# Attention pairs laid out anew: score units, row maxima, additions and softmax pieces of a mixture kernel

## Chip, cores and metric

The kernel runs on one core of a Trainium2 chip. The metric is device time in microseconds (us), the median of 3 runs. TensorE (PE) multiplies matrices, VectorE (DVE) reduces and does elementwise work, ScalarE (ACT) does exponentials and copies, GpSimd (POOL) does elementwise work between SBUF tiles, SyncE (SP) issues the DMAs in order. All engines run their own instruction queue in program order and wait for each other by semaphores.

## The reference, cut to what matters

```python
q_pool = q.reshape(B, H, S // 2, 2, D).mean(axis=3)      # B, H, S, D = 4, 8, 1152, 64
scores = (1 / np.sqrt(D)) * np.matmul(q_pool, k.transpose(0, 1, 3, 2))
scores = scores - np.max(scores, axis=-1, keepdims=True)
attn = np.exp(scores)
attn = attn / (np.sum(attn, axis=-1, keepdims=True) + 1e-09)
x = np.matmul(attn, v)            # then heads side by side: x is [2304, 512]
...
logits = x @ phi                  # 8 experts of 4 slots: softmax over tokens (d), over slots (c)
slot_input = d.T @ x
slot_out[e] = np.maximum(slot_input[e] @ w1[e], 0.0) @ w2[e]
y = c @ slot_out
...
xn = y / np.sqrt(np.mean(y * y, axis=-1, keepdims=True) + 1e-06) * rms_g
out = (silu(xn @ w_gate) * (xn @ w_val)) @ w_out
```

The gated layer's weights come as 64-bit numbers. Inputs q, k and phi are drawn eight times larger than the rest.

## The kernel before, in words

The 32 heads are handled in 16 pairs, p = 0 to 15. For a pair, the keys come in 9 tiles of 128 (kt) and the 576 pooled queries in two halves h of 288. One **score unit** (`qk`) multiplies a key tile with a half of the queries, for both heads at once: the high and low parts of k and q in three products, and a fourth (`pick` by `mr`) that adds minus the row maximum. ACT takes the exponential (`e`), `add_e` adds the tiles up for the softmax denominator (`acc`), and `av` multiplies them with the values. Row maxima of the next pair are found beforehand: a **maximum item** (`max_item`, 11 or 14 in a pair) multiplies q and k into two PSUM banks (`mxp`) and DVE reduces them (`mx`). `max_red` joins the pieces, `max_row` turns the column of maxima into a row on PE (`mxt`) and copies it on ACT (`mrow`), and `send_row` sends it by four small DMAs into `mr`, where the next pair's first score unit reads it.

Score units, maximum items and nearly all other products of this stage share three PSUM buffers of two banks each (`two_banks`), used in turn; a product waits until the reader of the buffer's last tenant is done. Two further banks hold the value products.

The order on every engine is written out by hand. For each pair the loop goes through its steps u: 9 steps of both halves, or, for pair 0 (`HALVED`), 18 steps, the first half's nine and then the second's. Within a step a short list such as `STEP` gives the order of score units (q), maximum items (m), additions (e) and, in every third step, a **visit**, the value products of the last three key tiles (a, b, c). `MAX`, `MAX_1` and `MAX_0` say how many maximum items each step may take. All other work is hung in by time: the tables `AT`, `AT_0` (pair 0), `AT_01` and `AT_15` give each piece a place such as 5.8 (within step 5, at eight tenths of its list), and `side` sorts them.

```python
while todo and todo[0][0] <= now + i / len(order) / len(steps) * 9:
    todo.pop(0)[2]()
```

Pieces that matter here: `round_k` and `high_q` (ACT) round k and q to their high parts, `low_k` and `low_q` (DVE) take the rest; `block_q` (ACT) fills the small stack `tb` for the last 64 rows of queries; `sum_q` (POOL) pools the queries. `load_64`, `abs_64` (ACT) and `turn_64` (DVE, called a **turn** below) fetch a block of 64-bit weights and make it 32-bit; `spill` sends it back to memory. `c_turn`, `c_exp`, `c_sum`, `c_out` make the softmax over slots, in pairs 6 and 7, 10 and 11, 14 and 15, and once after the pairs. `sums`, `recips` and `inverse` make the denominators of the pair before, `x_turn`, `x_divide`, `x_logits`, `logit_add` and `d_turn` its output and logits. `kraw`, `qraw`, `vt`, `kh`, `kl` and the raw 64-bit blocks share a pool of 11 buffers (A). After the pairs come the experts and the gated layer, which the change does not touch.

Of the kernel before, what the change touches and what calls it, by code (L numbers as in the profile page):

```python
# [13 lines left out]
AF = mybir.ActivationFunctionType  # L14
ALU = mybir.AluOpType
AX = mybir.AxisListType
PSUM = bass.MemoryType.PSUM

NP = 16
# [4 lines left out]
NBK = 6  # L24
TB = 96
# [4 lines left out]

STEP = "q0 m q1 m e0 e1".split()
STEP_V = "q0 q1 m e0 e1 a m m b c".split()
STEP_0 = "q m m e a b c".split()
VISIT = 3
PART = 6
MAX = [0, 0, 3, 0, 0, 3, 0, 0, 3]
MAX_1 = [1, 1, 3, 1, 0, 3, 0, 0, 3]
NMAX = 9
AHEAD = 3
AT = dict(  # L40
# [13 lines left out]
    recips=2.87,  # L54
    c_turn=8.74,
    c_exp=0.9,
    c_soft=[6.5, 8.9],
    pair_up=6.6,
    inverse=[3.4, 4.0],
    turn_64=[0.9, 5.8, 5.81],  # L60
    low_q=3.2,
    high_q=5.51,
    block_q=5.52,
# [17 lines left out]
    load_15=[0.5, 1, 1.5, 2, 2.5, 3, 3.5, 4, 4.5, 5.5, 5.84, 6, 6.5, 7, 7.5, 8, 8.5],  # L81
)
AT_0 = dict(
    max_tail=[2.85, 2.86],
    load_v=7.3,
    round_k1=[1.06, 1.56],
    block_q1=2.6,
    low_k=[1.3, 1.8],
    low_q=2.3,
    high_q=6.19,  # L90
    block_q=8.95,
    round_k=[7.91, 8.72],
    max_red=8.6,
    max_row=8.78,
    send_row=8.79,
    load_q=4.3,
    load_k=5.73,
    sum_q=5.91,
)
AT_01 = dict(  # L100
    x_turn=8.85,
# [1 line left out]
    drop_x=8.88,  # L103
    d_exp=8.84,
)
AT_15 = dict(
    x_turn=5.8,
    x_divide=[5.81, 5.82],
# [1 line left out]
    sums_a=8.55,  # L110
    inverse_a=[8.56, 8.57],
)
MAX_0 = [2, 1, 1, 1, 1, 0, 1, 1, 1, 1, 1, 1, 1, 1, 1, 1, 0, 0]
HALVED = (0,)
SQ_DVE = (0, 2)
SP_ACT = (1, 5, 4, 3, 2)
# [28 lines left out]
def attention_softmoe_gated_kernel(ctx: ExitStack, tc: tile.TileContext, kT, qT, vv, ip, cst, w1, w2, wg, wv, wo, rg, out):  # L145
# [263 lines left out]

    def add_e(p, kt, h):  # L410

        j = int(kt >= PART)
        n, e = kt - PART * j, ets[p, kt, h]
        if n == 0:
            first[p, h, j] = e
            return
        if n == 1:
            acc[p, h, j] = B([128, 2, HQ], F32, "acc")
        eng = dv if p in (0, NP - 1) and kt % 2 == 0 else gp
        eng.tensor_tensor(out=acc[p, h, j], in0=first[p, h, j] if n == 1 else acc[p, h, j], in1=e, op=ALU.add)  # L420

    def av(p, kt, h):
# [185 lines left out]
        ac.activation(ct[b], ct[b], AF.Exp)  # L608

    def c_sum(b):  # L610
        sm = csum[b] = S([TB, NBK], "csm")
        dv.reduce_sum(out=sm, in_=ct[b], axis=AX.X)
        ac.activation(sm, sm, AF.Copy, bias=1e-9)
        dv.reciprocal(sm, sm)

    csum = {}

# [101 lines left out]
    def side(p):  # L719
        n, m, l = p + 1, p + 2, p - 1  # L720
        todo = []

        def at(name, g):
            ts = (AT_0 if p == 0 else AT_15 if p == NP - 1 else AT_01 if p > 1 and p % 4 < 3 else AT).get(name, AT.get(name))
            for i, t in enumerate(ts if isinstance(ts, list) else [ts]):
                todo.append((t, len(todo), (lambda i=i: g(i))))

        if p == 0:
            at("round_k1", lambda i: round_k(1, i))
            at("block_q1", lambda i: block_q(1))  # L730
        if n < NP:
            at("low_k", lambda i: low_k(n, slice(576 * i, 576 * i + 576)))
            at("low_q", lambda i: low_q(n))
            at("load_v", lambda i: load_v(n))
            if p:
                at("max_tail", lambda i: max_item(n, NMAX + i))
            at("max_red", lambda i: max_red(n))
            at("max_row", lambda i: max_row(n))
            at("send_row", lambda i: send_row(n))
        if m < NP:  # L740
            at("load_q", lambda i: load_q(m))
            at("load_k", lambda i: load_k(m))
            at("sum_q", lambda i: sum_q(m))
            at("high_q", lambda i: high_q(m))
            at("block_q", lambda i: block_q(m))
            at("round_k", lambda i: round_k(m, i))
        if l >= 0:
            at("take_x", lambda i: take_x(l))
            at("sum_up", lambda i: sum_up(l, 1 - i))
            at("sums", lambda i: sums(l))  # L750
            at("recips", lambda i: recips(l))
            at("x_turn", lambda i: x_turn_all(l))
            at("x_divide", lambda i: x_divide(l, range(3 * i, 3 * i + 3)))
            at("drop_x", lambda i: rel("B"))
            at("inverse", lambda i: inverse(l, i))
            at("x_logits", lambda i: x_logits(l))
            at("logit_add", lambda i: logit_add(l))
            if p % 4 == 0 and p < NP - 1:
                at("d_turn", lambda i: dpart.__setitem__(("d", l // 4), (d_turn(l // 4), d_neg(l // 4))))
                at("d_exp", lambda i: d_exp(l // 4, *dpart.pop(("d", l // 4))))  # L760
            if p % 4 == 1 and p > 1:
                b = p // 4 - 1
                at("d_back", lambda i: d_back(b))
                at("d_copy", lambda i: d_copy(b))
                at("slot_part", lambda i: slot_part(b))
                at("slot_copy", lambda i: slot_copy(b))
                at("slot_turn", lambda i: slot_turn(b, pt[:, b]))
            if p % 4 == 2 and p > 2:
                b = p // 4 - 1
                at("c_turn", lambda i: c_turn(b))  # L770
            if p % 4 == 3 and p > 3:
                b = p // 4 - 1
                at("c_exp", lambda i: c_exp(b))
                at("c_soft", lambda i: (c_sum, c_out)[i](b))
        if p == 2:
            at("pair_up", lambda i: pair_up())
        if 0 < p < NP - 2:
            at("load_64", lambda i: load_64() if i < 2 or p % 2 or p < 8 else None)
            at("load_ew", lambda i: load(1, 99, KEEP_C + min(len(doubles), 4 * HELD + HELD_O)) if p >= FIRST_EW else None)
        if p < NP - 1:  # L780
            at("spill", lambda i: spill())
            at("abs_64", lambda i: abs_64(1))
            at("turn_64", lambda i: turn_64(1))
        if p == NP - 2:
            spill()
            assert not doubles
            at("load_14", lambda i: (keep_b.__setitem__(0, KEEP[3]), load(1, KEEP_A[0])))
        if p == NP - 1:
            at("sums_a", lambda i: sums(p))
            at("inverse_a", lambda i: inverse(p, i))  # L790
            at("load_15", lambda i: (keep_b.__setitem__(0, KEEP[0]), load(1, KEEP_A[1])))
        return sorted(todo, key=lambda x: x[:2])

    with tc.manual_schedule():
# [47 lines left out]
        def next_max(p, mx):  # L842
            if p == 0:
                mx += 9
                if mx < 14:
                    max_item(0, mx)
                    if mx == 13:
                        max_red(0)
                        max_row(0)
                        send_row(0, 3)  # L850
                else:
                    max_item(1, mx - 14)
            elif p == 1:
# [5 lines left out]
        for p in range(NP):  # L859
# [2 lines left out]
            steps = [(kt, h) for h in range(2) for kt in range(NKT)] if p in HALVED else [(kt, None) for kt in range(NKT)]  # L862
            for u, (kt, h) in enumerate(steps):
                now = u / 2 if p in HALVED else u
                order = STEP_0 if h is not None else STEP_V if kt % VISIT == VISIT - 1 else STEP
                quota = min(sum((MAX_0 if p == 0 else MAX_1 if p == 1 else MAX)[:u + 1]),
                            0 if p == NP - 1 else NMAX - AHEAD if p == NP - 2 else 99)
                for i, step in enumerate(order):
# [206 lines left out]
        c_turn(3)  # L1075
        c_exp(3)
        c_sum(3)
        c_out(3)
        for e in range(NE):
            pull()  # L1080
# [214 lines left out]
```

## Time and profile before

| | |
|---|---|
| median of 3 runs | 730.64 us (730.15 to 731.27) |
| profiled execution | 732.41 us, its span 730.3 us |
| busy: PE, DVE, POOL, ACT | 693.3, 478.9, 430.7, 393.6 us |
| pairs 0 to 15 | from 16.31 us to about 473 us of the span |
| a pair from 2 to 14 | 26 to 30 us |

Times in the profile are counted from the start of the span. A matmul's busy time includes its pipeline, so starts tell more than durations: in the timeline a row merges instructions of one kind that follow each other, gives the start, the length and how often, and in brackets the idle time of its engine just before and what ended it. PE is busy for 95% of the span, so most of what there is to see lies in short stops of PE and in stretches at the lower clock.

### The profile page before, as it was taken

The numbers are of one execution on the slowest core, as the hardware profiler recorded it, in microseconds if no ns is written. First come the engines' busy times: TensorE is split into PE (matmuls) and PEld (weight loads), VectorE is DVE, ScalarE is ACT, GpSimd is POOL, SyncE is SP. The second block draws the span as 40 slices with busy tenths as digits, with TensorE's granted clock in tenths as the row PEclk, the third lists the DMA queues.
The fourth block names the chain that finished last, engine by engine and source line by source line (L and its number), as shares of the span: only waits on it lengthen the run. The fifth ranks groups of instructions, "written<-read, shape, count | busy, mean of one in ns | idle before, by whom it ended". The sixth has DMA issues, their size and how long they took to land.

```text
span 730.3 us, 15136 instructions
## 1 busy us (share of the span) xinstructions
PE 693.3 (95%) x5924; PEld 484.6 (66%) x5924; DVE 478.9 (66%) x668; ACT 393.6 (54%) x828; POOL 430.7 (59%) x347
## 2 busy tenths in 40 slices
PE   4989999999999899999999999879999999999998
PEld 2666676666666566666666667434367888888887
DVE  5868898897797797788888775531064755534420
ACT  2455666656656666565665545342166865454320
POOL 5338788778687587686787775321026855535320
PEclk9999999999999999999999999979999999999999
DMA  5212633844835716527416317379990100000010
GB/s 176 98 57 98 213 115 115 285 140 147 282 112 178 247 54 243 190 68 272 145 41 243 104 47 263 114 245 373 388 353 1 44 15 29 30 30 29 15 37 35
DMA packets 52853, 103.53 MB, mean 142 GB/s; under 512 B 5816, under 2 KB 19632, under 8 KB 52784
## 3 DMA queue, kind: packets, MB, share of 16 engines
q1 hardware_dynamic: 52784, 102.59, 40.5%
q8 instruction: 46, 0.75, 0.4%
q14 instruction: 23, 0.19, 0.1%
HBM read 89.39 MB, written 13.11 MB: 140 GB/s over the span
## 4 chain that ended last, share of the span: by engine, by line
PE 78%; DVE 12%; DMA 4%; ACT 3%; issue 2%; POOL 1%; SPq 0%; DVEq 0%; ACTq 0%
PE yo L1198 21%; PE sc L403 18%; PE av L426 17%; PE mxp L346 4%; PE gv L1150 3%; DVE mx L347 3%; DVE kl L310 3%; DVE w L710 2%; PE hin L966 2%; DMA kraw<-in_kT_dram 2%; PE xo L488 2%; PE so L989 2%; PE sums L451 1%; PE mxp L356 1%; DVE mx L353 1%
## 5 line engine op out<-in xcount | busy, mean ns | idle before, releaser
L420 POOL TENSOR_TENSOR acc<-acc,e 128x576 f32<-128x576 f32 x148 | 207.9, 1433 | 37.2 <-ACT e L405 32.6
L405 ACT ACTIVATE e<-sc 128x576 f32<-128x576 f32 x288 | 165.0, 656 | 77.3 <-PE sc L403 76.7
L347 DVE TENSOR_REDUCE mx<-mxp 128x2 f32<-128x1024 f32 x120 | 143.5, 1221 | 62.7 <-PE mxp L346 62.7
L426 PE MATMUL av<-e,vt 128*64 128x288 f32 x1152 | 166.7, 417 | 0.0
L420 POOL TENSOR_TENSOR acc<-e 128x576 f32<-128x576 f32 x64 | 97.3, 1539 | 92.0 <-ACT e L405 91.8
L426 PEld LDWEIGHTS av<-e,vt 128*64 128x64 f32 x1152 | 73.4, 137 | 63.6 <-issue 27.6
L403 PE MATMUL sc<-qh,kh 64*128 64x288 f32 x576 | 95.4, 326 | 4.7 <-ACT e L405 3.9
L1198 PE MATMUL yo<-woh,hA 128*128 128x512 f32 (+1 forms) x312 | 98.9, 384 | 0.0
L403 PE MATMUL sc<-mr,pick 64*128 64x288 f32 x576 | 87.1, 295 | 1.9 <-DMA mr<-mrow 1.9
L403 PE MATMUL sc<-qh,kl 64*128 64x288 f32 x576 | 86.5, 295 | 0.0
L403 PE MATMUL sc<-ql,kh 64*128 64x288 f32 x576 | 86.5, 294 | 0.0
L1155 DVE SCALAR_TENSOR_TENSOR th<-th,gv 128x384 f32<-128x384 f32 x72 | 39.9, 554 | 62.5 <-ACT th L1152 61.8
L1181 POOL TENSOR_TENSOR hA<-hu,hA 128x384 fp32r<-128x384 f32 x48 | 48.7, 1016 | 42.7 <-ACT hA L1180 39.0
L403 PEld LDWEIGHTS sc<-qh,kh 64*128 64x128 f32 x576 | 55.0, 186 | 26.5 <-issue 7.4
L1198 PEld LDWEIGHTS yo<-woh,hA 128*128 128x128 f32 x312 | 57.6, 188 | 10.2 <-issue 0.7
L1152 ACT ACTIVATE th<-gv 128x384 f32<-128x384 f32 x72 | 35.2, 489 | 42.6 <-PE gv L1150 38.6
L1198 PE MATMUL yo<-wol,hA 128*128 128x512 f32 (+1 forms) x151 | 57.9, 383 | 0.0
L403 PEld LDWEIGHTS sc<-mr,pick 64*128 64x128 f32 x576 | 55.8, 187 | 2.4 <-DMA mr<-mrow 2.4
L403 PEld LDWEIGHTS sc<-qh,kl 64*128 64x128 f32 x576 | 55.7, 189 | 0.3
L403 PEld LDWEIGHTS sc<-ql,kh 64*128 64x128 f32 x576 | 55.6, 187 | 0.0
L346 PE MATMUL mxp<-kh,qh 64*128 64x512 f32 x240 | 48.8, 438 | 0.0
L1157 DVE SCALAR_TENSOR_TENSOR hu<-th,gv 128x384 f32<-128x384 f32 x72 | 39.9, 554 | 8.4 <-DVE th L1155 0.5
(190 smaller groups left out, 1065.4 us busy)
## 6 DMA issues: line engine op xcount, KB each, us to landing
w<-in_w_dram SPq DMA_DIRECT2D x86, 256.0 KB
w<-in_w_dram SPq DMA_DIRECT2D x21, 512.0 KB
vt<-in_vv_dram SPq DMA_DIRECT2D x16, 576.0 KB
qraw<-in_qT_dram SPq DMA_DIRECT2D x15, 576.0 KB
kraw<-in_kT_dram SPq DMA_DIRECT2D x15, 576.0 KB
away<-w SPq DMA_DIRECT2D x32, 256.0 KB
w<-away SPq DMA_DIRECT2D x32, 256.0 KB
raw<-in_wg_dram SPq DMA_DIRECT2D x12, 512.0 KB
```

What stands on the lines that cost most here:

```text
L310: eng.tensor_tensor(out=kl[p][:, c], in0=kraw[p][:, c], in1=f(kh[p][:, c]), op=ALU.subtract)
L346: pe.matmul(o[:, s, :], lhsT=q[r, 128 * t:128 * t + 128], rhs=k[r, 512 * c:512 * c + 512], start=True, stop=True)
L347: dv.reduce_max(out=heads[:, :, t, c], in_=o, axis=AX.X)
L403: pe.matmul(o[:, s, 0:HQ], lhsT=w[r, wk], rhs=q[r, c], start=(i == 0), stop=(i == 3))
L405: ac.activation(ets[p, kt, h], o[:, :, 0:HQ], AF.Exp, scale=0.0625)
L420: eng.tensor_tensor(out=acc[p, h, j], in0=first[p, h, j] if n == 1 else acc[p, h, j], in1=e, op=ALU.add)
L426: pe.matmul(avt[p, h][64 * s:64 * s + 64, 0:HQ], lhsT=vt[p][:, kt, 64 * s:64 * s + 64], rhs=ets[p, kt, h][:, s], start=(kt == 0), stop=(kt ...
L1152: ac.activation(t, o[0], AF.Tanh, scale=0.5)
L1155: dv.scalar_tensor_tensor(out=t, in0=t, scalar=1.0, in1=o[0], op0=ALU.add, op1=ALU.mult)
L1157: dv.scalar_tensor_tensor(out=u, in0=t, scalar=0.5, in1=o[1], op0=ALU.mult, op1=ALU.mult)
L1181: gp.tensor_tensor(out=b, in0=u, in1=f(a), op=ALU.subtract)
L1198: pe.matmul(o, lhsT=x, rhs=w[:, c], start=(ft == 0 and i == 0), stop=(ft == NF - 1 and i == 2))
```

## The change

Pair 0: the lists become "q e" for two steps and "q e m a m m b m c" for the third, so that three score units follow each other and all maximum items lie in the visits (`MAX_0`). All additions of pair 0 go to GpSimd (before, every second key tile's went to VectorE). The row of pair 0 itself is turned at the step after its second visit (`row_0`), not in the step of its last item; `round_k1`, `block_q1`, `low_k`, `low_q`, and the maxima of pair 1 (`max_red`, `max_row`, `send_row`) get other places. Pair 1: the twelve items lie in the visits but for one (`MAX_1`, `STEP_1`), and `max_red` comes at 5.83. All pairs: the accumulator of the first half is split after key tile 5 instead of 6 (`PART`); `c_sum` becomes three pieces at their own places (sum on DVE, guard on ACT, inverse on DVE); of the turns that stood at 5.8 and 5.81 one goes to 0.91 of the next pair, except in pairs 5, 9 and 13; pairs 8 and 10 may fetch a third 64-bit block.

```diff
 STEP = "q0 m q1 m e0 e1".split()
 STEP_V = "q0 q1 m e0 e1 a m m b c".split()
-STEP_0 = "q m m e a b c".split()
+STEP_1 = "q0 q1 m e0 e1 a m m b m c".split()
+STEP_0 = "q e".split()
+STEP_0V = "q e m a m m b m c".split()
-PART = 6
+PART = 5, 6
-MAX_1 = [1, 1, 3, 1, 0, 3, 0, 0, 3]
+MAX_1 = [0, 1, 4, 0, 0, 4, 0, 0, 3]
...
 AT = dict(
...
-    c_soft=[6.5, 8.9],
+    c_soft=[3.45, 5.505, 6.5, 8.52],
...
-    turn_64=[0.9, 5.8, 5.81],
+    turn_64=[0.9, 0.91, 5.8],
...
 AT_0 = dict(
-    max_tail=[2.85, 2.86],
     load_v=7.3,
-    round_k1=[1.06, 1.56],
-    block_q1=2.6,
-    low_k=[1.3, 1.8],
-    low_q=2.3,
-    high_q=6.19,
-    block_q=8.95,
-    round_k=[7.91, 8.72],
-    max_red=8.6,
-    max_row=8.78,
-    send_row=8.79,
+    round_k1=[0.6, 1.6],
+    block_q1=1.62,
+    low_q=2.1,
+    row_0=2.97,
+    low_k=[3.6, 5.1],
     load_q=4.3,
     load_k=5.73,
     sum_q=5.91,
+    high_q=6.19,
+    max_red=7.3,
+    max_row=7.48,
+    send_row=7.49,
+    round_k=[7.6, 8.6],
+    block_q=8.95,
 )
...
+AT_1 = dict(AT_01, turn_64=[0.9, 5.8, 5.81])
+AT_P1 = dict(max_red=5.83)
...
-MAX_0 = [2, 1, 1, 1, 1, 0, 1, 1, 1, 1, 1, 1, 1, 1, 1, 1, 0, 0]
+MAX_0 = [0, 0, 4, 0, 0, 4, 0, 0, 3, 0, 0, 3, 0, 0, 2, 0, 0, 0]
...
-        j = int(kt >= PART)
-        n, e = kt - PART * j, ets[p, kt, h]
+        j = int(kt >= PART[h])
+        n, e = kt - PART[h] * j, ets[p, kt, h]
...
-        eng = dv if p in (0, NP - 1) and kt % 2 == 0 else gp
+        eng = dv if p == NP - 1 and kt % 2 == 0 else gp
...
     def c_sum(b):
-        sm = csum[b] = S([TB, NBK], "csm")
-        dv.reduce_sum(out=sm, in_=ct[b], axis=AX.X)
-        ac.activation(sm, sm, AF.Copy, bias=1e-9)
-        dv.reciprocal(sm, sm)
+        csum[b] = S([TB, NBK], "csm")
+        dv.reduce_sum(out=csum[b], in_=ct[b], axis=AX.X)
+
+    def c_guard(b):
+        ac.activation(csum[b], csum[b], AF.Copy, bias=1e-9)
+
+    def c_inverse(b):
+        dv.reciprocal(csum[b], csum[b])
...
-            ts = (AT_0 if p == 0 else AT_15 if p == NP - 1 else AT_01 if p > 1 and p % 4 < 3 else AT).get(name, AT.get(name))
+            ts = (AT_0 if p == 0 else AT_15 if p == NP - 1 else AT_P1 if p == 1 else AT if p % 4 == 3 else AT_1 if p % 4 == 1 else AT_01).get(name, AT.get(name))
...
+            at("row_0", lambda i: (max_row(0), send_row(0, 3)))
...
-                at("c_soft", lambda i: (c_sum, c_out)[i](b))
+                at("c_soft", lambda i: (c_sum, c_guard, c_inverse, c_out)[i](b))
...
-            at("load_64", lambda i: load_64() if i < 2 or p % 2 or p < 8 else None)
+            at("load_64", lambda i: load_64() if i < 2 or p % 2 or p < 11 else None)
...
                     if mx == 13:
                         max_red(0)
-                        max_row(0)
-                        send_row(0, 3)
...
-                order = STEP_0 if h is not None else STEP_V if kt % VISIT == VISIT - 1 else STEP
+                if kt % VISIT < VISIT - 1:
+                    order = STEP if h is None else STEP_0
+                else:
+                    order = STEP_0V if p == 0 else STEP_1 if p == 1 else STEP_V
```

## Rows read from the trace of the kernel before

**Rows 1.** Waits of PE, whole span: us in total, times, longest us

```profile
PE sc L403 <- ACT e L405: 3.9, 2, 2.2
PE lgt L531 <- DVE mx L347: 2.8, 3, 0.9
...
PE sc L403 <- DMA mr<-mrow: 1.9, 2, 1.4
...
PE lgt L599 <- POOL acc L420: 1.0, 1, 1.0
...
PE xo L488 <- DVE mx L347: 0.9, 1, 0.9
PE lgt L599 <- DVE mx L347: 0.9, 1, 0.9
```

**Rows 2.** Windows of pairs 0, 1, 2, and two short ones: busy by engine, PEclk, DMA

```profile
16.31:48.00 31.69, 29.86 (x256) 19.77 (x256) 24.40 (x30) 15.36 (x29) 13.02 (x9) 1.00 0.16 57
48.00:79.79 31.79, 29.59 (x273) 20.23 (x271) 25.21 (x28) 17.29 (x33) 21.29 (x16) 0.95 0.39 131
79.79:106.08 26.29, 26.29 (x268) 18.00 (x267) 22.70 (x26) 17.32 (x34) 21.93 (x18) 1.00 0.42 133
...
51.66:55.06 3.40, 3.40 (x29) 3.26 (x27) 2.36 (x2) 1.83 (x4) 0.85 (x1) 0.50 0.96 330
242.85:246.25 3.40, 3.40 (x15) 1.40 (x14) 1.67 (x2) 2.98 (x10) 3.40 (x4) 0.51 0.93 297
```

**Rows 3.** Timeline of pair 7: start, length, engine, line, tiles, count, idle before

```profile
241.09 0.21 ACT L613 ACTIVATE csm<-csm 96x6 f32<-96x6 f32 x1 [2.24 <-DVE csm L612]
...
241.88 0.40 PE L403 MATMUL sc<-qh,kh 64*128 64x288 f32 x2 [2.19 <-ACT e L405]
```

**Rows 4.** Timeline of pair 3 at its last visit, and of pair 9 there

```profile
129.95 3.47 DVE L347 TENSOR_REDUCE mx<-mxp 128x2 f32<-128x1024 f32 x3
...
131.22 0.86 PE L488 MATMUL xo<-cs,xu 128*96 128x128 f32 x6 [0.94 <-DVE mx L347]
...
300.32 1.23 DVE L347 TENSOR_REDUCE mx<-mxp 128x2 f32<-128x1024 f32 x1 [1.98 <-PE mxp L346]
```

**Rows 5.** Durations by line: count, then ns minimum/median/maximum

```profile
L310 DVE TENSOR_TENSOR kl<-kraw,kh x30: 744/748/1989, 23.3 to 439.3; 128x576 fp32r<-128x576 f32 x30
...
L710 DVE SCALAR_TENSOR_TENSOR w<-w,raw x36: 672/683/1898, 71.3 to 436.8; 128x512 uint32<-128x512 uint32 x36
...
L420 POOL TENSOR_TENSOR acc<-acc,e x148: 1392/1412/1942, 24.8 to 459.9; 128x576 f32<-128x576 f32 x148
```

**Rows 6.** Timeline from the end of pair 0 into pair 1, all engines

```profile
46.13 0.33 PE L370 MATMUL mxt<-cs,mxw 128*128 128x128 f32 x1
...
50.98 0.40 PE L403 MATMUL sc<-mr,pick 64*128 64x288 f32 x1 [0.52 <-DMA mr<-mrow]
...
51.73 0.38 SPq L271 DMA_DIRECT2D kraw<-in_kT_dram  x1
...
58.08 0.67 ACT L285 CAST kh<-kraw 128x576 fp32r<-128x576 f32 x1 [1.33 <-DMA kraw<-in_kT_dram]
```

**Rows 7.** Timeline of PE in pair 0, one group of three steps

```profile
27.06 1.68 PE L426 MATMUL av<-e,vt 128*64 128x288 f32 x12
28.67 0.40 PE L403 MATMUL sc<-qh,kh 64*128 64x288 f32 x2
28.91 0.29 PE L403 MATMUL sc<-qh,kl 64*128 64x288 f32 x2
...
29.30 0.39 PE L346 MATMUL mxp<-kh,qh 64*128 64x512 f32 x2
...
31.98 1.68 PE L426 MATMUL av<-e,vt 128*64 128x288 f32 x12
```

**Rows 8.** Timeline of pair 1 at its second visit, VectorE and PE

```profile
70.88 0.18 DVE L365 TENSOR_REDUCE mxw<-mx 128x9 f32<-128x27 f32 x1
...
71.22 0.33 PE L370 MATMUL mxt<-cs,mxw 128*128 128x128 f32 x1
```

More of the change, by code (lines that the diff above doesn't have):

```diff
@@ L1077, in attention_softmoe_gated_kernel @@
         c_sum(3)
+        c_guard(3)
+        c_inverse(3)
         c_out(3)
```

## Prediction

> **What bounds the kernel now.** PE is the engine that sets the end. I read first PE's waits over the whole span, then windows pair by pair, then the timelines around each stop. The waits show six stops of 0.9 to 1.0 us of a small product (`lgt`, `xo`) for VectorE's maxima, 5.6 us in all; two stops of score units for an exponential, 3.9 us; and one place where a score unit waits for the row `mr`, 1.9 us [rows 1]. The windows show that pairs 0 and 1 take 31.7 and 31.8 us where pair 2, which does no less for its own scores and values, takes 26.3 without a gap, and that the granted clock is 0.5, the 1.2 GHz of the two levels, for 3.4 us of pair 1 and for 3.4 us of pair 7, both times after PE had stopped for about 2 us [rows 1 to 3]. A stretch of 3.4 us at half speed costs 1.7 us. So the change has to be judged at four places: inside pair 0, in pair 1, at the last visit of the later pairs, and in pairs 7 and 11.
>
> **Pairs 7 and 11: the softmax pieces.** In pair 7 ACT stands for 2.24 us before the guard (L613), since VectorE has two turns and two `low_k` in its queue before the sum; behind the guard in ACT's queue are the exponentials, all three PSUM buffers are full, and PE stops for 2.19 us [rows 3]. The clock falls right after it [rows 2]. The other stop of the same kind, 1.7 us (3.9 less 2.2) [rows 1], I place in pair 11, the other pair inside the loop with these lines; no fall of the clock follows it. After the change the sum stands at 3.45, behind `low_q` and one `inverse` only, and the guard two steps later: about 6 us for 0.3 us of work. ACT then waits for nothing. The inverse at 6.5 has the guard behind it, and `c_out` moves from 8.9 to 8.52, where ACT has only the casts of a 64-bit block before it. Nothing is late next that PE needs. Gain 3.9 plus 1.7 for the clock: 5.6 us; if the clock falls in pair 7 anyway, 3.9.
>
> **Last visits: the turns.** In pair 3 VectorE begins the three maxima of the last visit only at 129.95, takes 1.16 us for each, and PE, which needs the buffer of the first one back, stops for 0.94 us [rows 4]. In front of them stand two turns and two `low_k`. A turn takes 0.67 to 1.90 us, a `low_k` 0.74 to 1.99; the high ends are those that run beside a GpSimd addition, which itself goes from 1.39 to 1.94 [rows 5]. Pair 9, which has one turn there, lets VectorE idle 1.98 us before the first of these maxima [rows 4]. The change takes one turn away, so VectorE comes 0.67 to 1.90 us earlier; the six stops of this kind [rows 1] need 0.94. Also, with the first half split after tile 5, the two additions of step 5 become one in step 5 and one in step 6, which ends GpSimd's run about 1.4 us earlier and leaves the remaining turn or a `low_k` alone. At the least 0.67 each is won, 4.0 us; at most 5.6. I take 5.0. The turn goes to the start of the next pair, where VectorE has the two additions of `sum_up` (0.75 each, as a `low_k`) and then nothing until the first visit, over 3 us after the pair's start (six score units of 0.53): 0.7 us more fits in this cover. Without that cover it would delay the first visit's maxima by 0.7. A turn that comes later keeps its raw block in pool A longer. By the code a pair that starts with two turns open has three free buffers instead of four: the raw block and `qraw` get those of `kh` and `kl`, and `kraw` must wait for `vt`, that is for the last value product. SP issues `kraw` at about the pair's start then instead of some 4 us before it. In pair 1 it took 6.35 us from the issue of `kraw` to the `round_k` that needs it, with more than a megabyte in front of it [rows 6]. With nothing in front I expect some 4 to 4.5, and ACT reaches `round_k` 4.2 us after the start: no cost, see the rival.
>
> **Pair 0.** The front of the kernel is the same, so the first unit starts at 16.31 again. A unit alone takes four parts of 0.13 us; after value products the first part takes 0.24, so 0.53 and 0.63 [rows 7]. One group of three steps takes 4.92 us now (27.06 to 31.98) [rows 7]. By PE alone the new group needs 1.7 for the units, 1.61 for the values, 0.7 for three maxima and about 0.35 for the five more changes between maxima and values (0.07 each, an estimate from the 0.11 above): 4.4 us. But the maxima now come in a bunch, through three buffers, and VectorE needs 1.16 us each [rows 4] and has `low_q` and two `low_k` (0.74 to 1.99 [rows 5]) between them. Visit by visit, the larger of both: first 4 of about 0.9 and `low_q`, 4.4 to 5.6; then one short, `max_red` and three wide with a `low_k`, 4.9 to 6.1; then three with a `low_k`, 4.4 to 5.5; then PE's 4.6 (one item has eight small products). Sum 18.3 to 21.8; I take 19.9, each of the three at 1.2, since GpSimd is now busy most of the time. The first three units cost 2.9, at the low clock. After the last maxima come a visit (2.6), the turn of rows (0.3), three units (1.7) and values (1.7): 6.3. So pair 0 takes 2.9 + 19.9 + 6.3 and 0.3 for `high_q`, behind which ACT waits for `sum_q`: 29.4 instead of 31.7. Gain 2.3, bounds 0 and 4.1. The additions: 14 at 1.41 and `sum_q` at 1.4 make 21.1 us on GpSimd, within 29. The last one ends about 1.2 us into pair 1, where VectorE's `sum_up` waits for it; the first maxima there come at 1.7, so this costs nothing yet. `block_q1` now comes before the last item of pair 0, which so multiplies by pair 1's stack: one maximum piece is of other numbers, at equal time. `row_0` is turned 4.9 us before the second half's first unit needs it; the row of pair 1 took 4.85 [rows 6]: no cost.
>
> **Pair 1.** Its row is turned behind the second last visit's values, some 4.1 us before the fourth part of the first unit needs it. Turn to landing took 4.85 us, some of it in ACT's queue [rows 6]: the wait goes from 1.9 to between 0 and 0.7, I take 0.1, and the clock holds. Starting from pair 2's 26.3 [rows 2], pair 1 has three more maximum items, each a 0.22 us product and a change on either side (0.33, an estimate): 1.0 us. Two new waits come in. First, `kraw` of pair 3 can be issued only behind `send_row`; its `round_k` stands in ACT's queue before the denominators' copy `srow`, and `sumt` waits for that. Now it is ready 10 us into the pair, when PE is still held up by the row. Then it is ready about 7.4 us in, with `round_k` and two casts (2.0 us) and `srow` 9.8, and PE wants it at 8.5: a stop of 1.0 to 1.3, bounds 0 and 2.2; I take 1.1. Second, `max_red` at 5.83 comes behind `x_logits`, `logit_add`, the turn and the fourth maximum of this visit, while `max_row` still stands first in step 6. Now the row is turned 0.16 us after `max_red` ends [rows 8], with no room to spare. VectorE will need 0.45 to the first maximum, 4 by 1.16, 0.4 for the multiply (half of a 0.75 us operation), a turn of 0.67 to 1.90 and 0.18: 6.3 to 7.6 us from the visit's start; PE is there after about 5.4. A stop of 0.9 to 2.2; I take 1.4, short of the 2 us after which the clock fell. Pair 1: 26.3 + 1.0 + 0.1 + 1.1 + 1.4 = 29.9, gain 1.9; without the two stops 4.4, with a fall of the clock 0.2.
>
> **The sum.** 5.6 + 5.0 + 2.3 + 1.9 = 14.8 us. The profiled execution took 732.4 us, 2.1 more than its span and 1.8 more than the median. 732.4 - 14.8 = 717.6, which stands to a median as 715.8. The experts' weights are loaded as buffers come free, so their loads move with the pairs. Predicted 716 us.
>
> **Rivals.** (1) The new stops of pair 1 don't come and pair 0 runs at PE's pace: 5.6 + 5.6 + 4.1 + 4.4 = 19.7, 711 us. For it: each stop hangs on a microsecond of lead. Against: 0.16 us now [rows 8]. (2) The last visits stay late, because a `low_k` of 1.99 takes the turn's place: 5.0 lost, 721 us. Against: pair 9's 1.98 us of idle [rows 4]. (3) The softmax stop stays, ACT waiting at 5.505: 721 us; VectorE has six microseconds for it, so little speaks for it. (4) GpSimd becomes the bound of pair 0: if `low_q`, `low_k` and additions hold each other up (1.99 and 1.94 [rows 5]), GpSimd needs 14 by 1.94, 27.2, and `sum_q`, ends 4 us or more late, VectorE's `sum_up` and the maxima of pair 1 behind it come late, and PE stops for 2 us with a fall of the clock: 3.7 lost, 720 us. The Trainium skill (GPSIMD Engine Reference, Engine selection) rules that elementwise work with two inputs goes to VectorE, being about twice slower on GpSimd; by that rule this case holds, and the trace agrees on the ratio, 1.41 against 0.75. (5) Slower: `kraw` lands late in each pair that starts with two turns open (some seven). PE wants `srow` 7.9 us after the start, 2.4 us after `round_k` can start, so it decides if `round_k` starts later than 5.5 us after the pair's start. At 7.7, PE stops 2.2 us and loses 1.7 to the clock in each: 27 us, 743 us. Above about 6.9 us the whole gain is gone. Against: the megabyte that made the 6.35 us [rows 6] is missing.
>
> **How the numbers follow.** Forecast 0.52 (its own range 713 to 720), rival 1 0.15, rival 2 0.15, rival 3 0.05, rival 4 0.08, rival 5 0.05. The range, 710 to 722.5, holds all but rival 5 and the far ends of 1 to 4. Three runs tell 0.2% from no change: faster 0.94, same 0.02 (rival 5 halfway), slower 0.04.
>
> **What would show it.** No wait of ACT before L613's work; no stop of `xo` or `lgt` for the maxima; pair 0 about 29.4 us with units three by three; no wait for `mr` and full clock in pairs 1 and 7; stops of about a microsecond before `sumt` and before `mxt` in pair 1. The prediction is wrong if PE waits for exponentials early in later pairs with ACT at `round_k`.

## The result, and the profile after

| | before | after |
|---|---|---|
| median (lowest to highest) of 4 runs each | 730.95 us (730.15 to 731.49) | 723.41 us (722.65 to 725.93) |
| profiled execution, its span | 732.41, 730.3 us | 725.93, 723.8 us |
| pairs 0 and 1 | 63.5 us | 64.5 us |
| pairs 2 to 14 | 365.0 us | 358.8 us |
| pair 15 and what follows | 285.5 us | 284.3 us |

The ratio is 0.990, with a 95% interval of 0.988 to 0.992. The kernel is faster by 7.5 us, which is half of the forecast 14.8, and 723.4 lies just above the range. The profiled executions differ by 6.5 us, and the table places them: pairs 2 to 14 gain 6.2 us where 10.6 (5.6 + 5.0) were forecast, and pairs 0 and 1 lose 1.0 us where a gain of 4.2 (2.3 + 1.9) was forecast. The last 1.2 us lie in pair 15 and the work behind it; no run separates what made them. The profiled execution of the kernel after is the slowest of its four, 2.5 us above their median, so what is read from it below is read from its bad end.

First PE's waits over the whole span of the kernel after, to be read beside [rows 1] (us in total, times, longest us):

```profile
PE mxp L363 <- ACT srow L458: 3.9, 3, 1.8
...
PE mxt L374 <- DVE mxw L369: 1.9, 1, 1.9
...
PE sc L407 <- DVE mx L351: 1.0, 1, 1.0
...
PE mxp L337 <- ACT tb L304: 0.6, 1, 0.6
```

The two stops for exponentials (3.9 us), the six stops of `xo` and `lgt` for maxima (5.6 us) and the wait for `mr` (1.9 us) [rows 1] are all gone. In their place stand three stops behind ACT's `srow` (3.9 us), one before `mxt` in pair 1, which turns the row of pair 2 (1.9), one for the first maxima of pair 1 (1.0) and one for `tb` in pair 0 (0.6). The windows show where they lie. They are pairs 0, 1, 2, 4 and 8 of the kernel after, and two short stretches (columns as in [rows 2]):

```profile
16.27:47.16 30.89, 29.74 (x255) 18.55 (x254) 19.76 (x25) 14.71 (x28) 19.48 (x14) 1.00 0.17 59
47.16:80.72 33.56, 30.08 (x273) 19.82 (x271) 23.53 (x27) 17.21 (x34) 22.85 (x17) 0.95 0.42 140
80.72:107.03 26.31, 26.31 (x267) 18.00 (x265) 20.81 (x27) 17.30 (x34) 21.79 (x18) 1.00 0.39 125
133.81:162.75 28.94, 27.18 (x272) 18.08 (x271) 23.50 (x31) 17.21 (x34) 22.28 (x16) 1.00 0.58 192
244.79:275.19 30.40, 28.68 (x271) 19.07 (x270) 23.49 (x30) 17.36 (x34) 22.33 (x16) 0.94 0.54 182
...
71.14:74.55 3.41, 3.41 (x34) 3.41 (x32) 0.59 (x1) 1.95 (x3) 1.41 (x2) 0.50 0.03 6
255.46:258.87 3.41, 3.41 (x26) 2.35 (x23) 2.39 (x3) 0.72 (x2) 0.00 (x0) 0.50 0.43 155
```

Pair 2 has no gap, as before. Pair 1 holds 3.5 us of idle PE (33.56 less 30.08) and 3.4 us at 1.2 GHz; pairs 4 and 8 hold 1.8 and 1.7 us of idle, and the clock falls in pair 8. Pairs 4 and 8 took 27.9 us each before; they became slower while pairs 3, 6, 7, 10 and 11 became faster, by 1.25, 1.07, 3.95, 1.01 and 1.97 us, and pair 12 by 0.37.

The timeline of pair 7 of the kernel after, where [rows 3] showed ACT standing before the guard:

```profile
236.71 0.68 DVE L718 SCALAR_TENSOR_TENSOR w<-w,raw 128x512 uint32<-128x512 uint32 x1
...
237.31 3.42 ACT L409 ACTIVATE e<-sc 128x576 f32<-128x576 f32 x6 [0.46 <-PE sc L407]
...
240.01 0.17 DVE L622 RECIPROCAL csm<-csm 96x6 f32<-96x6 f32 x1
```

ACT runs six exponentials in a row at the place where it stood for 2.24 us. The timeline from the last visit of pair 3 into pair 4, which answers to [rows 4]:

```profile
129.26 1.23 DVE L351 TENSOR_REDUCE mx<-mxp 128x2 f32<-128x1024 f32 x1 [0.16 <-PE mxp L350]
130.93 0.86 PE L492 MATMUL xo<-cs,xu 128*96 128x128 f32 x6
133.92 0.34 SPq L275 DMA_DIRECT2D kraw<-in_kT_dram  x1
...
141.37 0.67 ACT L289 CAST kh<-kraw 128x576 fp32r<-128x576 f32 x1 [3.27 <-DMA kraw<-in_kT_dram]
143.06 0.40 ACT L458 ACTIVATE srow<-sums 128x288 f32<-128x288 f32 x1
143.51 0.33 PE L363 MATMUL mxp<-kh,tb 128*128 128x128 f32 x1 [1.76 <-ACT srow L458]
```

VectorE now waits for PE at the last visit (0.16 us) and `xo` follows without a stop. But `kraw` is issued at 133.92, which is 0.11 us after pair 4 began, and its 576 KB are there only at 141.37. ACT stands for 3.27 us at `round_k`; behind it in ACT's queue is `srow`, and PE stops for 1.76 us. This is the start of rival 5.

`kraw` is issued 0.11 us after the start in six pairs (3, 4, 5, 8, 9 and 12), but it is not as late in all of them. ACT begins `round_k` 7.6 and 7.5 us after the start in pairs 4 and 8, 6.1 in pairs 3 and 12, and 4.2 and 4.6 in pairs 5 and 9, where PE loses nothing. The windows of the 5 us before the start of pair 4 and of pair 5 show what differs:

```profile
128.81:133.81 5.00, 5.00 (x40) 2.55 (x37) 4.52 (x6) 2.79 (x5) 5.00 (x4) 1.00 0.74 237
157.75:162.75 5.00, 5.00 (x39) 2.18 (x36) 4.61 (x8) 1.72 (x4) 4.90 (x4) 1.00 0.90 305
```

`vt`, the raw block and `qraw` (576, 512 and 576 KB, 1.7 MB) are asked for in about this time. At 237 GB/s 1.2 MB of them had come in pair 4, at 305 GB/s 1.5 MB in pair 5, so that in pair 4 more was still under way when `kraw` was issued.

### The profile page after: what moved, and what is told of

It is laid out like the page before. It is cut to its first block, busy times and chain, and to the rows that moved or that the text cites. A ratio compares the mean times of both kernels' runs of the same rounds, so it can differ in the third digit from the quotient of the medians.

```text
span 723.8 us, 15142 instructions
## 1 busy us (share of the span) xinstructions
PE 692.3 (96%) x5924; PEld 482.5 (67%) x5924; DVE 459.5 (63%) x663; ACT 393.1 (54%) x828; POOL 435.3 (60%) x352
## 4 chain that ended last, share of the span: by engine, by line
PE 85%; DMA 6%; DVE 3%; ACT 3%; issue 2%; POOL 0%; SPq 0%; ACTq 0%; DVEq 0%; POOLq 0%
PE yo L1210 21%; PE sc L407 20%; PE av L430 20%; PE mxp L350 4%; PE gv L1162 4%; DMA kraw<-in_kT_dram 3%; DMA w<-away 2%; PE hin L976 2%; PE xo L492 2%; PE so L999 2%; PE xl L509 1%; PE sums L455 1%; PE mxp L360 1%; PE x L1027 1%; PE pp L569 1%
## 5 line engine op out<-in xcount | busy, mean ns | idle before, releaser
L424 POOL TENSOR_TENSOR acc<-acc,e 128x576 f32<-128x576 f32 x154 | 216.4, 1425 | 44.5 <-ACT e L409 40.3
L430 PE MATMUL av<-e,vt 128*64 128x288 f32 x1152 | 168.7, 418 | 0.2 <-ACT e L409 0.2
L424 POOL TENSOR_TENSOR acc<-e 128x576 f32<-128x576 f32 x63 | 93.6, 1495 | 74.7 <-ACT e L409 74.6
```

The source lines that it names most:

```text
L430: pe.matmul(avt[p, h][64 * s:64 * s + 64, 0:HQ], lhsT=vt[p][:, kt, 64 * s:64 * s + 64], rhs=ets[p, kt, h][:, s], start=(kt == 0), stop=(kt ...
```

## The experiments

My theory after the result: the gain was given back at three places, which don't depend on each other. Among the pairs that start with two turns open, `kraw` comes too late in 4, 8 and 12. In pair 1, `max_row` stands too early for the maxima before it, PE stops and the clock falls. In pair 0 the layout has little to win. The rivals are named at each run. All ratios are to the kernel before, run on the same chip.

**e1, `kraw` first.** By the code `kraw`, the raw block and `qraw` are issued in this order: raw at 0.1, `qraw` at 0.3, `kraw` at 0.31 of a pair. The edit puts the keys first, so that the free buffer goes to `kraw` and the raw block is the one that waits. The rival was that the transfers themselves are too slow in any order.

```diff
-    load_q=0.3,
-    load_k=0.31,
+    load_q=0.06,
+    load_k=0.05,
```

> The changed kernel with one thing moved: in each pair the loads of kraw and qraw are asked for ahead of the raw 64-bit block, so kraw takes the buffer of kh (free after the pair's last score unit) and the raw block takes that of vt. Theory (late buffer): the stops of PE before the last maximum item for srow in pairs 4, 8 and 12 (1.76, 1.72 and 0.37 us) go, with the fall of the clock in pair 8: 3.9 to 5.6 us less than the changed kernel's 723.4, 718 to 719.5. Rival (the DMA engines are the limit and kraw is slow whenever it is asked for beside the experts' weights): ACT still waits for kraw at round_k in pairs 4 and 8, and the time stays within 1 us of 723.

Measured: 721.16 us, ratio 0.985 (0.984 to 0.987). In the timeline of e1 the same stretch as above reads:

```profile
130.12 0.47 SPq L275 DMA_DIRECT2D kraw<-in_kT_dram  x1
...
134.44 0.38 SPq L666 DMA_DIRECT2D raw<-in_wv_dram  x1
...
138.49 0.68 ACT L289 CAST kh<-kraw 128x576 fp32r<-128x576 f32 x1
...
142.11 0.22 PE L363 MATMUL mxp<-kh,tb 128*128 128x128 f32 x1
```

`kraw` is issued 4.2 us before pair 4 starts at 134.33, the raw block waits in its place, and neither ACT nor PE stops. Pairs 4, 8 and 12 take 26.9 us each, and pairs 2 to 14 together 352.46, which is 6.4 us less than after and 12.6 less than before. So the late buffer is what the moved turns had brought, and the rival falls. The time gains less than was expected: from 0.990 to 0.985, some 3.6 us. In part the stops in the profile of after were large ones: e2, e5, e6 and e11 below leave the order of the loads and the later pairs as after, and in their profiles these pairs take 355.7, 355.6, 355.8 and 358.5 us, with stops of 1.0 to 2.6 us in pair 8 and of 0 to 1.3 us in pair 4. Against the 352.5 of e1 the late `kraw` thus costs 3.2 to 6.4 us, differently in each execution.

**e2, the row turned later in pair 1.** Only the turn of the row in pair 1 moves (it is the row of pair 2), from the head of step 6 to behind the first score units of that step. The rival: PE loses the same time at the next product that needs the buffers.

```diff
-AT_P1 = dict(max_red=5.83)
+AT_P1 = dict(max_red=5.83, max_row=6.6, send_row=6.61)
```

> The changed kernel with max_row and send_row of pair 1 at 6.6 instead of 5.95 and 6.0, so the row of pair 2 is turned two score units later. Theory: the stop of 1.92 us before the turn goes and with it the fall of the clock in pair 1 (1.7 us): 719.8. Rival: the clock falls in pair 1 anyway, or VectorE's delay shows up at the next visit: 721.5 to 723.4.

Measured: 721.02 us, 0.987 (0.984 to 0.989). PE's waits from 60 to 440 us of e2:

```profile
PE mxp L363 <- ACT srow L458: 2.3, 2, 1.3
PE mxt L374 <- DVE mxw L369: 0.7, 1, 0.7
```

The stop before `mxt` falls from 1.92 to 0.7 us, the clock holds, and pair 1 takes 31.0 us instead of 33.56. That is 1.2 from the stop and 1.7 from the clock, less some 0.4 that comes in elsewhere in the pair. The rival falls by the trace; in the time the interval still touches that of after (0.988 to 0.992).

**e3, the softmax pieces alone.** The kernel before, with `c_sum` split in three as in the change, at its places, and nothing else. This asks whether the 5.6 us stand by themselves or whether the turns are needed for them.

```diff
-    c_soft=[6.5, 8.9],
+    c_soft=[3.45, 5.505, 6.5, 8.52],
...
```

> The kernel before with the softmax sum in three pieces at 3.45, 5.505 and 6.5 (and the output at 8.52), nothing else. Theory: the stops of 2.19 and 1.71 us in pairs 7 and 11 and the fall of the clock in pair 7 go, 5.6 us less than 730.9: 725.3. Rival: with the stop gone the two turns make VectorE late at the last visits of these pairs as in the others, 0.95 us each, and only 3.7 us are won: 727.2.

Measured: 728.89 us, 0.996 (0.994 to 0.997). PE's waits from 60 to 440 us of e3:

```profile
PE lgt L531 <- DVE mx L347: 2.8, 3, 0.9
PE xo L488 <- DVE mx L347: 2.5, 3, 1.0
```

No stop for an exponential is left and the clock holds in pair 7. But a PE that isn't stopped reaches the late maxima of the last visit sooner: in pairs 7 and 11 new stops of 0.99 and 0.54 us appear. The two pairs gain 4.25 us together, and 5.8 with these stops taken off. So this part alone is worth less than with the turns moved, where the pairs gain 5.9. The rival named this; the time gained, 2.5 us, is below both expectations.

**e4, the turns alone.** The kernel before with the turn moved to 0.91, `AT_1`, and the third block in pairs 8 and 10; `PART` and the softmax pieces as before.

```diff
-    turn_64=[0.9, 5.8, 5.81],
+    turn_64=[0.9, 0.91, 5.8],
...
+AT_1 = dict(AT_01, turn_64=[0.9, 5.8, 5.81])
...
```

> The kernel before with one turn moved from 5.81 to 0.91 of the next pair (not in pairs 5, 9, 13) and the third block in pairs 8 and 10, nothing else. Theory: the six stops of 0.94 us at the last visits shrink or go (4.0 to 5.6 us won; less if the split of the accumulator is needed too), but kraw is issued only at the pair's start and PE stops for srow in pairs 4, 8, 12 (3.9 us and perhaps a fall of the clock, 1.7): net 0 to -2, 729 to 731. Rival (the late kraw comes from another part of the change): no stop for srow, 725 to 727.

Measured: 728.09 us, 0.997 (0.995 to 1.000), hardly told from no change. PE's waits from 60 to 440 us of e4, without the two softmax stops, which stay (3.4 us):

```profile
...
PE mxp L360 <- ACT srow L455: 1.9, 2, 1.1
PE mxp L357 <- ACT srow L455: 1.4, 1, 1.4
PE lgt L532 <- DVE mx L348: 0.9, 2, 0.5
PE xo L489 <- DVE mx L348: 0.5, 1, 0.5
```

The moved turn takes the last-visit stops of pairs 6, 10 and 12 away and halves those of pairs 3, 4 and 8, to some 0.46 us each. So 1.4 of their 5.6 us stay. The `srow` stops come with the turn, which shows that they belong to this part, though in other pairs than after: 0.78, 1.13 and 1.40 us in pairs 3, 4 and 5, none in 8 and 12. What stays of the last-visit stops asks what `PART` does.

**e8, `PART` 6 for both halves.** The kernel after, but the split as before.

```diff
-PART = 5, 6
+PART = 6, 6
```

> The changed kernel with the accumulator of both halves split after key tile 6 as before. Theory (the split takes part in making VectorE free at the last visits): stops of about 0.45 us of xo or lgt come back in pairs 3, 4 and 8, as with the turns alone: 724 to 725. Rival (the turn alone does it, given the other parts): 723.4 as the changed kernel.

Measured: 726.98 us, 0.993 (0.990 to 0.995). PE's waits from 60 to 440 us of e8:

```profile
PE xo L492 <- DVE mx L351: 1.6, 3, 0.5
PE lgt L535 <- DVE mx L351: 0.9, 2, 0.5
```

Stops of about half a microsecond come back in five last visits (pairs 3, 4, 7, 8 and 11), 2.5 us in all. So the moved turn takes the stops of pairs 6, 10 and 12 by itself; in pairs 3, 4 and 8 the turn and the earlier split take about half each. What the split is worth in time stays open: the median is worse than both expectations, but the interval overlaps that of the kernel after, and the `srow` stops were only 0.5 and 0.4 us in the execution profiled here.

**e5, additions of pair 0 shared again.** The kernel after with every second addition of pair 0 on VectorE, as before. It tests rival 4, by which GpSimd is the wrong engine for them.

```diff
-        eng = dv if p == NP - 1 and kt % 2 == 0 else gp
+        eng = dv if p in (0, NP - 1) and kt % 2 == 0 else gp
```

> The changed kernel with pair 0's additions shared between VectorE and GpSimd as before (every second key tile on VectorE). Theory (the additions of pair 0 on GpSimd end late, VectorE's sum_up waits for them and the first maxima of pair 1 come late): the stop of 0.96 us of a score unit in pair 1 goes, pair 0 stays at about 31: 722.4. Rival (VectorE is the bound of pair 0): six additions of 0.75 us and more bring stops of 1 to 4 us into pair 0: 724.5 to 727.

Measured: 731.10 us, 0.998 (0.996 to 1.001): the whole gain is gone. The waits of VectorE from 17 to 57 us of e5, those of PE there, and a piece of its timeline:

```profile
DVE acc L424 <- POOL acc L424: 14.1, 6, 6.0
```

```profile
PE sc L407 <- DVE mx L351: 4.1, 5, 2.0
```

```profile
40.62 1.94 DVE L424 TENSOR_TENSOR acc<-acc,e 128x576 f32<-128x576 f32 x1 [1.30 <-POOL acc L424]
42.48 2.34 DVE L351 TENSOR_REDUCE mx<-mxp 128x2 f32<-128x1024 f32 x2
43.75 0.40 PE L407 MATMUL sc<-qh,kh 64*128 64x288 f32 x2 [1.96 <-DVE mx L351]
```

Each addition on VectorE needs the sum that GpSimd has just made. VectorE stands for it, 14.1 us in six waits, five of them with the maxima of a visit behind them in its queue and the longest, 6.0 us, for the last addition of pair 0; one of the additions then takes 1.94 us beside GpSimd's `sum_q`. PE, three buffers deep in maxima, stops five times, the clock falls for 6.8 us, and pair 0 takes 40.2 us. Neither theory had expected so much. The Trainium skill (GPSIMD Engine Reference, Engine selection) gives elementwise additions to VectorE, since GpSimd is about twice slower on two inputs; the durations here agree (1.41 against 0.75 us). The time is still better with all of them on GpSimd, 0.990 against 0.998 with every second one on VectorE, where the maxima stand behind them. All additions of pair 0 on VectorE, where no addition would wait for GpSimd, was not run.

**e6, pair 0 as before.** The kernel after with the whole of pair 0's lists, places and engines as before. It asks whether pair 0's part brings anything at all.

```diff
-STEP_0 = "q e".split()
-STEP_0V = "q e m a m m b m c".split()
+STEP_0 = "q m m e a b c".split()
+STEP_0V = "q m m e a b c".split()
...
-MAX_0 = [0, 0, 4, 0, 0, 4, 0, 0, 3, 0, 0, 3, 0, 0, 2, 0, 0, 0]
+MAX_0 = [2, 1, 1, 1, 1, 0, 1, 1, 1, 1, 1, 1, 1, 1, 1, 1, 0, 0]
...
```

> The changed kernel with the whole of pair 0 laid out as before (lists, maxima, additions, places, row of pair 0 in the step of its last item). Theory (the new layout of pair 0 brings under 1 us inside it, and takes the wait for mr away): pair 0 31.7 us; the wait for mr (1.9 us) and a fall of the clock come back in pair 1 beside the stop before the row's turn: 725 to 727. Rival (pair 0's part brings nothing even at the border, since pair 1 pays for it in other stops): 723 to 724.

Measured: 725.22 us, 0.991 (0.988 to 0.993), the same as after within the intervals. Pair 0 takes 31.3 us, and pair 1 rises from 33.56 to 35.9, since the wait for `mr` (1.39 and 0.52 us) with its fall of the clock comes back and the stop before `mxt` stays with its own. What pair 0's part brings is mostly seen in pair 1, and in the profiles alone: this execution had 3.1 us less than after in pairs 2 to 14, by smaller `srow` stops and without the fall in pair 8, and the medians don't tell the two kernels apart.

**e11, fewer changes in pair 0's visits.** The kernel after, but the maxima in two bunches. Theory: each change between maxima and values costs about 0.1 us, so fewer of them are faster. The rival: the maxima then wait for VectorE.

```diff
-STEP_0V = "q e m a m m b m c".split()
+STEP_0V = "q e m m a b m m c".split()
```

> The changed kernel with pair 0's visits in the order q e m m a b m m c: four changes between maxima and values in a visit instead of six. Theory (each change costs PE about 0.1 us and PE is the bound of pair 0): pair 0 about 0.8 us shorter, 722.6. Rival (VectorE and the three PSUM buffers are the bound): stops of 0.3 to 1 us for the maxima in the visits, pair 0 the same or longer, 723.4 to 725.

Measured: 723.84 us, 0.989 (0.987 to 0.991), no difference to after. Pair 0 of e11 in the windows:

```profile
16.85:48.52 31.67, 30.11 (x255) 19.00 (x254) 19.76 (x25) 14.65 (x28) 19.47 (x14) 1.00 0.16 57
```

The theory falls: PE is idle for 1.56 us here against 1.15 after, and its busy time less that of the low clock is 27.9 us in both.

**e7 and e9, the remedies together.** e7 has e1's order, the row in pair 1 turned later, a turn moved behind it, `block_q1` behind the item that had waited for it, and pair 1's `sum_up` moved behind the first maxima. e9 is the same without that last move. The cut shows e9; e7 has `sum_up=[1.5, 1.51]` in `AT_P1` besides.

```diff
...
-    block_q1=1.62,
+    block_q1=2.65,
...
-AT_P1 = dict(max_red=5.83)
+AT_P1 = dict(max_red=5.83, max_row=6.6, send_row=6.61, turn_64=[0.9, 0.91, 6.95])
```

> The changed kernel with the loads of kraw and qraw first, and in pair 1 the row of pair 2 turned at 6.6, the turn at 6.95 and sum_up at 1.5, block_q1 at 2.65. Theory (every stop found has its own cause): no stop over 0.5 us from 17 to 450 us, pair 1 29 us or less, pairs 4, 8 and 12 26.9: 5.5 from kraw, 3.6 from the row, 1.0 from sum_up, 0.6 from block_q1, together up to 10.7 less than the profiled execution of the changed kernel, 714 to 716 as a median. Rival (stops move on, and falls of the clock after the pairs take the rest): 718 to 720.

Measured for e7: 719.37 us, 0.982 (0.979 to 0.984). PE's waits from 47 to 80 us of e7:

```profile
PE sumt L465 <- DVE mx L351: 0.8, 1, 0.8
PE sums L455 <- DVE mx L351: 0.4, 1, 0.4
PE mxp L350 <- DVE mx L351: 0.4, 1, 0.4
```

The stop of 0.96 us at the first maxima became three, of 0.45, 0.44 and 0.80 us within one visit, and the clock fell behind them although none of the three reaches a microsecond. `sum_up` had only been moved from before the maxima to between them. The time is the rival's.

> The changed kernel with the loads of kraw and qraw first, in pair 1 the row of pair 2 turned at 6.6 and the turn at 6.95, and block_q1 at 2.65; sum_up stays where the change has it. Theory (sum_up at 1.5 had made VectorE late at the first visit of pair 1): the stops of 0.45, 0.44 and 0.80 us there shrink to the 0.96 and 0.37 us seen before, the clock holds in pair 1, which takes 30.3 us against 32.4: 717. Rival (the clock falls in pair 1 whatever the order): 719 to 720.

Measured for e9: 716.19 us, 0.979 (0.977 to 0.981), the lowest median of the study. The windows of pairs 0, 1, and 2 to 14 of e9:

```profile
16.14:46.27 30.13, 29.63 (x255) 18.40 (x254) 19.75 (x25) 14.60 (x28) 19.47 (x14) 1.00 0.17 60
46.27:76.64 30.37, 28.82 (x275) 18.40 (x273) 24.15 (x27) 17.03 (x34) 23.26 (x17) 1.00 0.38 125
76.64:429.13 352.49, 352.11 (x3551) 239.54 (x3549) 287.57 (x364) 224.48 (x443) 276.15 (x198) 1.00 0.49 169
```

The clock doesn't fall between 20 and 460 us, and PE is idle for 0.4 us in the thirteen pairs from 2 to 14.

**e10, `sum_up` of pair 0 on GpSimd.** e9 with the two additions that wait for GpSimd's last one given to GpSimd itself.

```diff
-        dv.tensor_tensor(out=acc[p, h, 0], in0=acc[p, h, 0], in1=acc.pop((p, h, 1)), op=ALU.add)
+        (dv if p else gp).tensor_tensor(out=acc[p, h, 0], in0=acc[p, h, 0], in1=acc.pop((p, h, 1)), op=ALU.add)
```

> The kernel of e9_joined_2 with pair 0's two sum_up additions on GpSimd. Theory (VectorE waits at sum_up for GpSimd's last additions, and the first maxima of pair 1 wait behind it): the stop of 0.96 us in pair 1 goes, pair 1 29.3 us: 716. Rival (GpSimd, 2.8 us further behind, makes the denominators or the exponentials' buffers of pair 1 late): 717 to 719.

Measured: 716.45 us, 0.979 (0.977 to 0.981). The stop of 0.96 us is gone and pair 1 takes 29.4 us instead of 30.4, but the time is that of e9. The microsecond won in pair 1 is smaller than what executions differ by in the clock (last section), so it isn't shown in the time.

**e12, the later pairs alone.** The lists, maxima, places and additions of pairs 0 and 1 as before, e1's order, all else as after.

> Pairs 0 and 1 as in the kernel before (lists, maxima, places, additions), the later pairs as in the changed kernel, with the loads of kraw and qraw first. Theory: the whole gain is of the later pairs (12 us: 5.9 of the softmax, 5.9 of the turns), pairs 0 and 1 31.7 and 31.8 us with the wait for mr and one fall of the clock: 719 to 720, and what the new pairs 0 and 1 bring at their best is the 2 to 3 us to e9_joined_2. Rival (kraw first is of no use in pair 1 there, or the old pair 1 takes more stops): 721 to 723.

Measured: 720.37 us, 0.984 (0.982 to 0.987). Pairs 2 to 14 take the same 352.46 us as in e1. So 10.8 of the 15.0 us by which e9 beats the kernel before (731.19 on that chip) belong to the later pairs and the order of the loads, and the other 4.2 to pairs 0 and 1, from whatever cause.

## Why the prediction was wrong, point by point

**Softmax pieces: right.** Forecast 5.6 us; pairs 7 and 11 gained 3.95 and 1.97, together 5.9. e3 adds that this holds only beside the moved turns.

**Turns at the last visit: right in mechanism, sized a little low.** Forecast 5.0 us, at most 5.6, with the six stops gone. With `kraw` out of the way, e1's pairs 3, 4, 6, 8, 10 and 12 are 1.45, 0.99, 1.07, 0.98, 1.01 and 1.01 us shorter than before, 6.5 in all; what lies above 5.6 the stops don't explain. Rival 2 fell. By e4 the turn alone takes three quarters of the six stops, so the split of the accumulator is the smaller part. One of the six, 1.0 us in pair 6, the profile puts down to a GpSimd addition and not to the maxima [rows 1]; it went with the others, in e4 too.

**What the turns cost: the step that failed first.** "With nothing in front I expect some 4 to 4.5, and ACT reaches `round_k` 4.2 us after the start: no cost". The issue at the pair's start was forecast rightly (0.11 us after it); the time from there was not: it held in pairs 5 and 9 (`round_k` at 4.2 and 4.6 us), but ACT could begin `round_k` only 7.6 us after the start in pair 4 (141.37 less 133.81), 7.5 in pair 8, and 6.1 in pairs 3 and 12. "With nothing in front" was wrong: of the 1.7 MB issued some 4 us ahead, about 0.5 MB had not come by the start of pair 4, by the windows shown. Rival 5 had the mechanism and its point, 5.5 us: past it PE stopped 1.76, 1.72 and 0.37 us in pairs 4, 8 and 12 (in pair 3 not), and the clock fell once. It was wrong in scale, with seven pairs and a fall in each. The sign named for it came, with the product behind `srow` in the place of the exponentials. Its bound of 6.9 us doesn't follow from its terms either: 14.8 us over seven pairs are 2.1 each, which is reached at 5.9 us with a fall and at 7.6 without. In the profiled execution, against e1, all this cost 6.4 us; in four others (e2, e5, e6, e11) 3.2 to 6.1. The later pairs were short by 4.4 (10.6 less 6.2): the turns won 1.5 and the softmax pieces 0.3 more than their terms, and 6.4 less these 1.8 is 4.6. I had treated the late `kraw` as a case that holds everywhere or nowhere, and so left it out of the range.

**Pair 1: the second step that failed.** The timeline of pair 1 of the kernel after:

```profile
48.96 1.43 DVE L443 TENSOR_TENSOR acc<-acc 128x576 f32<-128x576 f32 x2 [6.16 <-POOL acc L424]
51.58 0.40 PE L407 MATMUL sc<-qh,kh 64*128 64x288 f32 x2 [0.96 <-DVE mx L351]
...
67.73 1.30 DVE L718 SCALAR_TENSOR_TENSOR w<-w,raw 128x512 uint32<-128x512 uint32 x1
68.95 1.21 DVE L357 TENSOR_REDUCE mx<-mxp 128x8 f32<-128x1024 f32 x1
70.20 0.18 DVE L369 TENSOR_REDUCE mxw<-mx 128x9 f32<-128x27 f32 x1
70.53 0.30 PE L374 MATMUL mxt<-cs,mxw 128*128 128x128 f32 x1 [1.92 <-DVE mxw L369]
```

Forecast 29.9 us, measured 33.56. "A stop of 0.9 to 2.2; I take 1.4, short of the 2 us after which the clock fell": it was 1.92 us, inside the bounds, with the turn in front of the last maximum at 1.30 us, and the clock fell behind it at 71.14, which costs 1.7 us. "This costs nothing yet", of `sum_up` waiting for GpSimd's last addition: that addition ended 1.8 us into the pair instead of 1.2, and PE stopped for 0.96 us at 51.58. For the three more maximum items I took 1.0; PE's busy time less the 1.7 us of low clock is 28.4, which is 2.1 above pair 2, though no run shows that the items alone make it. Against that, the stop of 1.1 us for `kraw` hardly came (0.16 and 0.37 us), and the wait for `mr` went as forecast. 1.7 for the clock, 0.5 for the stop before `mxt`, 1.0 for the one at the first maxima, 1.1 for PE's work, less 0.6 for `kraw`, make 3.7, which is the difference. e2 confirms the first two of these, e10 the third.

**Pair 0: a term mis-sized.** Forecast 29.4 us against 31.7, measured 30.89. One group of the kernel after, beside [rows 7], and the item that waits for `block_q1`:

```profile
25.33 0.44 PE L337 MATMUL mxp<-kh,tb 128*128 128x384 f32 x1 [0.64 <-ACT tb L304]
...
33.81 0.40 PE L407 MATMUL sc<-qh,kh 64*128 64x288 f32 x2
...
36.01 0.71 PE L430 MATMUL av<-e,vt 128*64 128x288 f32 x4
36.64 0.50 PE L350 MATMUL mxp<-kh,qh 64*128 64x512 f32 x2
...
38.59 0.40 PE L407 MATMUL sc<-qh,kh 64*128 64x288 f32 x2
```

The group takes 4.78 us (33.81 to 38.59), against 4.92 before. From one group's first unit to the next, the last four groups take 1.55 us less than before together and the second takes 1.1 more (6.55 against 5.45). The clock comes up at 20.93 in the profile of before and at 19.94 in that of after; half of the time until then is lost, 2.3 and 1.8 us, and without it pair 0 takes 29.4 before (31.69 less 2.31) and 29.1 after (30.89 less 1.83). So the layout wins 0.3 us and the rest of the 0.8 is the clock's. My sum gave the new pair 1.2 us of low clock (2.9 less 1.7 for the first units) and compared it with a 31.7 that holds 2.3: 1.1 of the 2.3 us were no gain of the layout. Of the other 1.2, two stops in the second group took 1.0 that I had costed at nothing: 0.64 us at the item behind `block_q1`, and 0.36 at the unit behind `row_0`. With `block_q1` later (e7, e9, e10) pair 0 takes 28.5 to 28.8 us at the full clock, which is 0.6 to 0.9 less than before.

**GpSimd: rival 4 fell.** The 14 additions and `sum_q` took 21.2 us (21.1 forecast) and were not slowed by VectorE; e5 shows that sharing them as before undoes the gain in the new layout. But the late end that this rival named did come, 0.6 us later than I took, at the price of 0.96 us in pair 1.

**The sum.** In the profiled executions the later pairs are short by 4.4 us, pair 1 by 3.7 and pair 0 by 1.5, and 1.2 us come from pair 15 and behind it, which I had not counted: 14.8 less 8.4 is the 6.5 measured, but for rounding.

**What stays open.** That e9 lands near the forecast is no proof of it: pairs 2 to 14 gain 12.5 us there instead of 10.6, and pairs 0 and 1 gain 3.0 instead of 4.2. How much of the 4.2 us between the medians of e9 and e12 is the layout is not settled either: in the profiles pairs 0 and 1 differ by 4.1 us, 3.0 of which is the time that the clock took to come up in pair 0.

## What to carry to other kernels

When work is moved later, follow the buffers that it keeps and see which load then has to wait for them: order the loads so that the one whose reader comes first in some engine's queue gets the free buffer. Ask not only when a load is issued but how much of the loads before it is still under way then. Add up separately what a change does to work and what low clock lies in the time compared with, and where a stop is of about the size after which the clock fell, put a fall into the bounds. An engine that is slower at an operation can still be the better one, if nothing that another engine needs soon stands behind it in its queue.

## What the runs showed of the hardware

The clock fell to 1.2 GHz for 3.4 us behind a single stop of 1.92 us (pair 1) and one of 1.72 us (pair 8), but not behind one of 1.76 us (pair 4), all in one execution. Of the stop before `mxt` in pair 1, 1.92 us made it fall and 1.82 us in e8 did not; the two for `mr` (1.39 and 0.52 us) made it fall in the kernel before, and 1.30 and 0.52 in e12 did not. In e7 it fell behind three stops of 0.45, 0.44 and 0.80 us. So the length of the longest stop alone doesn't tell whether it falls. The time at which it first came up lay between 18.9 and 22.0 us of the span with the new pair 0 and between 20.3 and 24.9 with the old, on the same work each time. The later falls differ between executions as well: the part from pair 15 on takes 284 to 287 us, and 5.1 to 8.5 of these are lost to low clock. That is more than most single edits here. A two-input addition on VectorE took 0.75 us alone and up to 1.95 us beside one of GpSimd.
